# Phase one ordered by hand, h3T over hT, and values one chain later in a memory-augmented attention and mixer kernel

## The chip, the cores and the metric

The kernel runs on one core of a Trainium2 chip, in one launch. The metric is the device time in microseconds; each kernel's time is the median of several executions on the chip. TensorE (PE in the profile) multiplies matrices into PSUM; VectorE (DVE), ScalarE (ACT) and GpSimd (POOL) do the rest; SyncE (SP) only issues DMAs, and POOL issues some too. Each engine takes its instructions in the order in which they were written for it, and semaphores tie the engines together.

## The reference

x is 2048 tokens of 1024 numbers. Two branches read its layer norm: A, an attention over segments of 32 tokens with 8 memory tokens that the previous segment hands on, and B, a token-shift mixer with an MLP.

```python
def _A_ref(x, mem0, Wq, Wk, Wv, Wo, seg_len):      # 32 heads of 128
    for s in range(n_seg):
        h = jnp.concatenate([mem, x[:, s*seg_len:(s+1)*seg_len]], axis=1)
        q, k, v = (jnp.einsum('btd,dhe->bhte', h, W) for W in (Wq, Wk, Wv))
        scores = jnp.where(mask, jnp.einsum('bhqe,bhke->bhqk', q, k) * scale, -1e9)
        o = jnp.einsum('bhqk,bhke->bhqe', _softmax(scores), v)
        o = jnp.einsum('bhte,hed->btd', o, Wo)
        mem = o[:, :M]
        outs.append(o[:, M:])
def _B_ref(x, w1, w2, w3, w4):
    h = _gelu(_layernorm(x) @ w1)
    ...
    x1 = x + concat_of_four_shifted_quarters(h) @ w2
    return x1 + _gelu(_layernorm(x1) @ w3) @ w4
xn = _layernorm(x)
return x + _A_ref(xn, ...) + _B_ref(xn, ...)
```

## The kernel before

The kernel is written under a manual schedule: nothing reorders it, so the order of the program's lines is the order on each engine. It has four stages that follow one another on TensorE.

Phase one works on 16 tiles of 128 tokens. For each tile, `ln_stats` takes mean and variance on DVE and the power -0.5 on POOL; `ln_apply` (L205) normalises into `xn2` on DVE, issues the DMA transpose and the next loads on SP, and has ACT overwrite the tile `xts[n]` with its layer norm (L213). The first four tiles are transposed by TensorE against an identity (`pe_trans`, L228), with DVE copying one half out of PSUM and ACT the other. `stage1` (L246) multiplies w1 by the transposed tiles, for eight column blocks `co` of eight accumulating matmuls each, and ACT's GELU writes hTB; `seg_sums` (L240) adds up segments for branch A. The tiles go in nine groups: 1, 1, then 2 each. `warm` issues matmuls on a zero tile.

Phase two (L286) computes x1 tile by tile, 16 matmuls each, with the second layer norm `xn3`, written back to memory as R1 by POOL's queue, and transposed by DMA into xn3T through SP's queue. Between the transposes SP issues the twelve remaining loads of w3 (L309).

Phase three (L456) goes over four blocks `tb` of 512 tokens: 28 chains of eight matmuls (L461), each followed by a GELU into `h3T` (L462), then 56 chains' worth of matmuls with w4 (L479). h3T and w4 lie in a pool that is opened where phase two's pools were closed, so their memory is that of hTB, w2, the x tiles and phase two's ring.

The attention takes 32 steps, four blocks `b` of 512 tokens by eight groups `hg` of four heads. A step has twelve chains of eight matmuls (L799): four for q, four for k, four for v. Between them stands work of the step before, put there by `at(c, ...)`, after chain c: `scores(p, m)` (L565) multiplies q and k into psS, ACT takes the exponential (ET, L574), DVE makes normalised weights and lays them out as a block-diagonal matrix BD (L576 to L589); `values(p, m)` (L596) multiplies V by BD into psO, DVE adds a memory term into oX (L604), and ACT copies one column out, oTm (L608). There is one psS, one psO, three BD, and a ring of four PSUM tiles ("mm") for all chains. Step 1 of a block has the output projection of the block before (`out_chain`, L698). In block 0, `first_soft` and its companions treat the first segment.

## Time and profile before

| | us |
|---|---|
| median of 3 executions | 1581.95 |
| lowest and highest | 1572.84, 1586.62 |
| the profiled execution | 1586.39 |
| its span in the trace | 1584.6 |

Device time counts a little more than the span, which runs from the first to the last instruction. Times in the trace start at the span's start. Phase one runs from 0 to 85, phase two to 140, phase three from 140 to 560, the attention from 560 to the end. A row of a timeline gives start, duration, engine, line, operation, output <- inputs, shape and count, and in brackets the idle time before it with what ended it. A row of the waits gives who waited for whom, the sum in us, how often, and the longest.

### The profile page before, as it was taken

The page shows a single profiled execution, that of the slowest core. Times are in us where ns is not written, and L with a number is a line of the kernel's source. Part 1 is how long each engine was busy: PE and PEld are TensorE (multiplying, and loading weights), DVE is VectorE, ACT ScalarE, POOL GpSimd, SP SyncE. Part 2 cuts the span into 40 slices and gives each one's busy share as a digit, 9 for nine tenths or more (in the row PEclk, how much of TensorE's full clock was granted, in tenths as well). Part 3 has the DMA queues.
Part 4 walks back from the last instruction along what each step waited for, and adds up shares of the span by engine and source line. Part 5 has one row for each costly group of instructions (what it writes and reads, how often), then busy time and mean ns, then how long its engine had stood idle before and what let it go on. Part 6 is the DMA issues. An engine that isn't in the chain of part 4 may idle for free.

```text
span 1584.6 us, 24108 instructions
## 1 busy us (share of the span) xinstructions
PE 1525.0 (96%) x9609; PEld 793.9 (50%) x9609; DVE 667.9 (42%) x1562; ACT 460.4 (29%) x1249; POOL 232.7 (15%) x640
## 2 busy tenths in 40 slices
PE   7997999999999999999999999999999999999998
PEld 5953444444444466665544444444444444444445
DVE  6365011010110225566632666641666651566652
ACT  4632301202113024444410343420334420334320
POOL 3233010020120101212110111110111110111100
PEclk7999999999999999999999999999999999999999
DMA  5779644454220645464522454431445441344211
GB/s 154 192 199 254 218 158 135 133 199 133 73 100 22 205 136 171 134 186 141 166 84 63 133 154 140 136 112 47 133 140 153 134 129 54 110 133 133 94 32 38
DMA packets 190885, 208.38 MB, mean 132 GB/s; under 512 B 51176, under 2 KB 158712, under 8 KB 190768
## 3 DMA queue, kind: packets, MB, share of 16 engines
q1 hardware_dynamic: 183520, 182.49, 38.5%
q0 software_dynamic: 7248, 24.31, 4.3%
q8 instruction: 77, 1.26, 0.4%
q14 instruction: 40, 0.33, 0.1%
HBM read 170.07 MB, written 25.17 MB: 123 GB/s over the span
## 4 chain that ended last, share of the span: by engine, by line
PE 69%; DVE 18%; ACT 5%; issue 3%; DMA 3%; POOL 1%; SPq 0%; DVEq 0%; POOLq 0%; ACTq 0%
PE psP L698 14%; PE psV L548 12%; PE ps L479 12%; PE ps L461 12%; PE psK L541 5%; PE psQ L525 4%; ACT ET L574 4%; DVE Q L532 4%; PE ps L253 3%; DVE BD L589 3%; DVE oX L604 2%; DMA xn3T<-xn 2%; PE psO L600 1%; DVE EQ L576 1%; DVE PT L585 1%
## 5 line engine op out<-in xcount | busy, mean ns | idle before, releaser
L698 PE MATMUL psP<-wo_sb,oX 128*128 128x512 bf16 x1024 | 222.8, 379 | 0.0
L479 PE MATMUL ps<-w,h3T 128*128 128x512 bf16 x896 | 195.0, 379 | 0.0
L525 PE MATMUL psQ<-xT,w 128*128 128x512 bf16 x768 | 174.3, 379 | 0.0
L548 PE MATMUL psV<-w,xT 128*128 128x512 bf16 x768 | 173.8, 379 | 0.0
L541 PE MATMUL psK<-xT,w 128*128 128x512 bf16 x768 | 173.8, 379 | 0.0
L541 PEld LDWEIGHTS <-w 128*128 128x128 bf16 x1280 | 122.4, 98 | 90.0 <-issue 4.3
L698 PEld LDWEIGHTS <-oX 128*128 128x128 bf16 x1024 | 99.7, 98 | 118.4
L608 ACT CAST oTm<-psO 128x16 bf16<-128x16 f32 x128 | 22.9, 179 | 455.0 <-DVE oX L604 455.0
L525 PEld LDWEIGHTS <-w 128*128 128x128 bf16 x1024 | 97.7, 98 | 109.8
L462 ACT ACTIVATE h3T<-ps 128x512 bf16<-128x512 f32 x112 | 66.5, 597 | 288.8 <-PE ps L461 284.0
L574 ACT ACTIVATE ET<-psS 32x132 f32<-32x132 f32 x512 | 139.2, 272 | 4.6
L479 PEld LDWEIGHTS <-h3T 128*128 128x128 bf16 x896 | 87.2, 98 | 103.8
L548 PEld LDWEIGHTS <-xT 128*128 128x128 bf16 x768 | 74.1, 98 | 84.8
L591 POOL TENSOR_TENSOR BD<-ET,c_segone_sb 128x16 bf16<-128x16 f32 x128 | 33.7, 263 | 562.2 <-ACT ET L574 562.2
L461 PE MATMUL ps<-xn3T,w3a 128*128 128x512 bf16 x448 | 99.7, 384 | 13.4 <-ACT h3T L462 13.4
L532 DVE TENSOR_TENSOR Q<-psQ,QM 128x512 bf16<-128x512 f32 (+1 forms) x128 | 83.6, 678 | 65.0 <-ACT Q L531 40.4
L576 DVE STREAM_TRANSPOSE EQ<-ET 128x128 f32<-128x128 f32 x128 | 39.9, 311 | 164.2 <-ACT ET L574 164.2
L604 DVE TENSOR_TENSOR oX<-psO,VM 128x512 bf16<-128x512 f32 (+1 forms) x128 | 86.4, 675 | 48.2 <-PE psO L600 48.2
L549 ACT CAST V<-psV 128x512 bf16<-128x512 f32 x128 | 75.0, 586 | 99.8 <-PE psV L548 98.0
L461 PE MATMUL ps<-xn3T,w3b 128*128 128x512 bf16 x448 | 97.7, 379 | 0.0
L589 DVE TENSOR_TENSOR BD<-PT,c_segone_sb 128x512 bf16<-128x512 bf16 x128 | 89.9, 702 | 4.5
L392 DVE TENSOR_SCALAR xt<-xt,lnst 128x1024 bf16<-128x1024 bf16 x16 | 8.7, 546 | 196.9 <-POOL R L391 196.9
(149 smaller groups left out, 1558.7 us busy)
## 6 DMA issues: line engine op xcount, KB each, us to landing
w<-in_A_Wq_dram SPq DMA_DIRECT2D x32, 1024.0 KB, 5.7
w<-in_A_Wk_dram SPq DMA_DIRECT2D x32, 1024.0 KB, 5.7
w<-in_A_Wv_dram SPq DMA_DIRECT2D x32, 1024.0 KB, 5.7
R_scratch<-x POOLq DMA_DIRECT2D x16, 512.0 KB, 8.0
R<-R_scratch SPq DMA_DIRECT2D x16, 512.0 KB, 7.7
chunk<-in_A_Wv_dram SPq DMA_DIRECT2D x8, 1024.0 KB, 6.1
R_scratch<-R POOLq DMA_DIRECT2D x16, 512.0 KB, 6.7
chunk<-in_A_Wo_dram SPq DMA_DIRECT2D x8, 1024.0 KB, 6.0
```

What stands on the lines that cost most here:

```text
L461: nc.tensor.matmul(ps[:], w3[:, k, (f % FH) * P:(f % FH + 1) * P], xn3Ts[tb][:, :, k, :], start=(k == 0), stop=(k == KT - 1))
L462: nc.scalar.activation(h3T[:, f, :], ps[:], ACTF.Gelu_apprx_tanh)
L479: nc.tensor.matmul(ps[:], h3T[:, f, j * P:(j + 1) * P], w4t[f // 4][:, f % 4, ch * 512:(ch + 1) * 512], start=(f == 0), stop=(f == FT - 1))
L525: nc.tensor.matmul(ps[:], w[:, k, hh * P:(hh + 1) * P], s.xm[:, k, 0:512], start=(k == 0), stop=(k == KT - 1))
L532: nc.vector.tensor_tensor(q3[:, j0:16, 0:SEG], p3_[:, j0:16, :], QM[:, 4 * s.hg + hh, z + j0:z + 16].unsqueeze(2).to_broadcast((P, 16 - j0 ...
L541: nc.tensor.matmul(ps[:, 0:c], w[:, k, hh * P:(hh + 1) * P], s.xm[:, k, h2 * c:(h2 + 1) * c], start=(k == 0), stop=(k == KT - 1))
L548: nc.tensor.matmul(ps[:], s.xm[:, k, m * P:(m + 1) * P], w[:, k, :], start=(k == 0), stop=(k == KT - 1))
L549: nc.scalar.copy(s.V[:, m, :], ps[:])
L574: nc.scalar.activation(ET[q, :, :], ps[q, :, W * j:W * (j + 1)], ACTF.Exp, scale=SCALE)
L589: nc.vector.tensor_tensor(B4[:, :, :, 0:SEG], PT[:].unsqueeze(2).to_broadcast((P, 4, 4, SEG)), so.unsqueeze(3).to_broadcast((P, 4, 4, SEG) ...
L604: nc.vector.tensor_tensor(oX[:, hsl(s.hg), m * P:(m + 1) * P].rearrange("p h (j i) -> p h j i", i=SEG)[:, :, j0:4, :], p4[:, :, j0:4, 0:SE ...
L698: nc.tensor.matmul(ps[:], oX[:, h, m * P:(m + 1) * P], wo_sb[:, h, ch * 512:(ch + 1) * 512], start=(h == 0), stop=(h == H - 1))
```

## The change

In phase one the tiles go in eight pairs. The first pair's matmuls are split: for six column blocks the first half of w1 (k 0 to 3) is used, then tiles 2 and 3 are transposed, then the second half follows. x2 and x3 are loaded between the halves of w1. A GELU on a one-column tile is ACT's first instruction. ACT's layer norm of the x tiles becomes a call of its own, `normalise_x`. Tiles 0 and 1 are transposed through the "mm" ring, 2 and 3 through one tile of two banks. The warm matmuls read a tile of 0.5 in place of zero, are 16 in place of 13, and two more follow each of the first two transposes. Three constants are loaded in phase two. The last four loads of w3 move from phase two to the start of phase three. hT gets a pool of its own that lives until the end of phase three, and h3T is a view of it. In the attention each `values` is called one chain later, behind the next `scores`; `first_soft`, `first_trans` and `out_chain` move by one chain with it.

```diff
+    load_qones, qones = const_tile("c_qones", ..., later=True)
+    load_causal, causal = const_tile("c_causal", causal_np, F32, later=True)
+    load_mask40, mask40 = const_tile("c_mask40", _mask40(False), later=True)
...
+    ht_pool = htx.enter_context(tc.tile_pool(name="hT", bufs=1))
+    hT_all = ht_pool.tile([P, KT * (S + 4)], BF16)
+    hTB = hT_all[:].rearrange("p (k s) -> p k s", k=KT)
+    h3T = hT_all[:, 0:FT * 512].rearrange("p (f s) -> p f s", f=FT)
...
-        hTB = keep.tile([P, KT, S + 4], BF16)
...
+            nc.vector.memset(fill[:], 0.5)
+            pre = ring.tile([P, 1], F32, tag="pre")
+            nc.scalar.activation(pre[:], fill[:, 0:1], ACTF.Gelu_apprx_tanh)
...
             load_x(0)
             load_x(1)
-            for k0 in (0, 4):
-                nc.sync.dma_start(w1_sb[:, k0:k0 + 4, :], w1_v[:, k0:k0 + 4, :])
-            for n in range(2, 8):
+            load_w1(0)
+            load_x(2)
+            load_x(3)
+            load_w1(4)
+            for n in range(4, 8):
                 load_x(n)
...
+            def w1_part(g, co, ps, ks):
+                for k in ks:
+                    nc.tensor.matmul(ps, w1_sb[:, k, co * P:(co + 1) * P], xn2Ts[g][:, :, k, :], start=(k == 0), stop=(k == KT - 1))
+                if ks[-1] == KT - 1:
+                    nc.scalar.activation(hTB[:, co, 2 + g * 256:2 + g * 256 + 256], ps, ACTF.Gelu_apprx_tanh)
...
+            warm(16)
             ln_stats(0)
+            ln_stats(1)
+            ln_apply(0)
+            pe_trans(0)
+            warm(2)
+            ln_apply(1)
+            pe_trans(1)
+            warm(2)
+            normalise_x(0)
+            normalise_x(1)
+            first = [mm_tile("ps1")[:, 0:256] for _ in range(4)]
+            t = aux_tile([P, 2, 512], "A", "ps1")
+            first += [t[:, 0, 0:256], t[:, 1, 0:256]]
+            for co in range(6):
+                w1_part(0, co, first[co], range(4))
+            ln_stats(2)
+            ln_stats(3)
+            for n in (2, 3):
+                ln_apply(n)
+            for n in (2, 3):
+                pe_trans(n)
+            for co in range(6):
+                w1_part(0, co, first[co], range(4, KT))
+            stage1(0, (6, 7))
+            seg_sums(0)
+            seg_sums(1)
+            ln_stats(4)
+            for g in range(1, NT // 2):
+                nxt = [n for n in (2 * g + 2, 2 * g + 3) if n < NT]
+                for n in nxt:
+                    if n + 1 < NT:
+                        ln_stats(n + 1)
+                    ln_apply(n)
+                    dma_trans(n)
+                stage1(g, range(4))
+                if g == 1:
+                    normalise_x(2)
+                    normalise_x(3)
+                for n in nxt:
+                    normalise_x(n)
+                stage1(g, range(4, KT))
+                seg_sums(2 * g)
+                seg_sums(2 * g + 1)
...
-                if n < 12:
+                if n < 8:
                     load_w3(4 + n)
+                elif n == 8:
+                    load_qones()
+                    load_causal()
+                    load_mask40()
...
-        h3T = big.tile([P, FT, 512], BF16)
+        for i in range(12, 16):
+            load_w3(i)
...
         if pp is not None:
-            at(0, values, pp, 3)
+            at(1, values, pp, 3)
         if p is not None:
             at(0, scores, p, 0)
             for m in range(3):
-                at(3 * m + 3, values, p, m)
                 at(3 * m + 3, scores, p, m + 1)
+                at(3 * m + 4, values, p, m)
...
-            values(p, 3)
             scores(s, 0)
+            values(p, 3)
...
```

DVE, phase one, from the first tile's normalisation on. Before, tile 1 (x_102) is normalised after the statistics of tile 2 (x_103); xn2T is the transposed tile.

```order
L210 TENSOR_SCALAR xn_169<-x_101,lnst 128x1024
L236 CAST xn2T<-psT 128x512
L187 BN_STATS st<-x_103 128x6 x2
L188 BN_AGGR lnst<-st 128x2
L190 TENSOR_SCALAR ab<-lnst 128x1
L191 TENSOR_SCALAR ab<-ab,lnst 128x1
L210 TENSOR_SCALAR xn_195<-x_102,lnst 128x1024
```

After:

```order
L218 TENSOR_SCALAR xn_174<-x_101,lnst 128x1024
L250 CAST xn2T<-psT 128x512
L218 TENSOR_SCALAR xn_193<-x_102,lnst 128x1024
L250 CAST xn2T<-psT 128x512
L202 BN_STATS st<-x_103 128x6 x2
L203 BN_AGGR lnst<-st 128x2
```

Tile 1 is normalised and copied before anything is asked of tile 2.

ACT, from phase two into phase three: the last normalisations xn, then the first GELUs, with what each waits for. Before:

```order
L305 ACTIVATE xn_1890<-x_1858,nm_1888,r_1886 128x1024 [waits DVE_49,DMAHW3_49,Activation_49,Pool_49]
L305 ACTIVATE xn_1926<-x_1894,nm_1924,r_1922 128x1024 [waits DVE_49,DMAHW5_49,Activation_49,Pool_49]
L462 ACTIVATE h3T<-ps_1965 128x512 [waits DMASW5_49,DMASW6_49,DMASW4_49,DMASW7_49,DMASW3_49,DMAHW0_49,DMASW2_49,DMAHW1_49,DMASW1_49,DMAHW2_49,DMASW0_49,DMAHW6_49,DVE_49,DMAHW7_49,PE_49,Activation_49]
L462 ACTIVATE h3T<-ps_1975 128x512 [waits PE_49]
L462 ACTIVATE h3T<-ps_1985 128x512 [waits PE_49]
```

After:

```order
L341 ACTIVATE xn_1780<-x_1748,nm_1778,r_1776 128x1024 [waits DVE_49,DMAHW0_49,Activation_49,Pool_49]
L341 ACTIVATE xn_1816<-x_1784,nm_1814,r_1812 128x1024 [waits DVE_49,DMAHW1_49,Activation_49,Pool_49]
L341 ACTIVATE xn_1852<-x_1820,nm_1850,r_1848 128x1024 [waits DVE_49,DMAHW2_49,Activation_49,Pool_49]
L503 ACTIVATE hT_all<-ps_1894 128x512 [waits PE_49]
L503 ACTIVATE hT_all<-ps_1904 128x512 [waits PE_49]
```

The first GELU's waits for DMA queues (DMAHW is SP's, DMASW is POOL's) and for DVE are gone; the normalisations ahead of it still wait for DMAs.

ACT, in the attention, a steady stretch of a step with chains for K and V. Before:

```order
L574 ACTIVATE ET<-psS 32x132 x4
L542 CAST K<-psK 128x512 x3
L608 CAST oTm<-psO 128x4x4
L574 ACTIVATE ET<-psS 32x132 x4
L542 CAST K<-psK 128x512
L549 CAST V<-psV 128x512 x2
```

After:

```order
L616 ACTIVATE ET<-psS 32x132 x4
L584 CAST K<-psK 128x512
L650 CAST oTm<-psO 128x4x4
L584 CAST K<-psK 128x512 x2
L616 ACTIVATE ET<-psS 32x132 x4
L584 CAST K<-psK 128x512
```

oTm stood directly ahead of the exponentials ET; now it stands one cast behind the previous ones, with two casts between it and the next.

More of the change, by code (lines that the diff above doesn't have):

```diff
@@ L105, in const_tile @@
         t = cpool.tile(list(arr.shape), dt, name=name + "_sb")
-        nc.gpsimd.dma_start(t[:], d.ap())
+        load = lambda: nc.gpsimd.dma_start(t[:], d.ap())
+        if later:
+            return load, t
+        load()
         return t
@@ L244, in seg_sums @@
                 nc.scalar.copy(xs[:, :, 4 * n:4 * n + 4], ps[:])
-            def stage1(gi, cos):
-                n0, nt = groups[gi]
-                xn2T = xn2Ts[gi]
-                w = nt * P
-                for co in cos:
-                    ps = mm_tile("ps1")
-                    for k in range(KT):
-                        nc.tensor.matmul(ps[:, :w], w1_sb[:, k, co * P:(co + 1) * P], xn2T[:, 0:nt, k, :], start=(k == 0), stop=(k == KT - 1))
-                    nc.scalar.activation(hTB[:, co, 2 + n0 * P:2 + n0 * P + w], ps[:, :w], ACTF.Gelu_apprx_tanh)
@@ L484 @@
                     att_prep()
+    htx.close()
     specx.close()
@@ L841 @@
             out_part(b, 2, 0, hp)
+            scores(s, 3)
             values(s, 2)
-            scores(s, 3)
             out_part(b, 3, 0, hp)
```

97 lines of the change are left out of this document (38 added, 59 removed).

## The prediction

> **What bounds the kernel now.** I read the page's busy line first, then TensorE's waits, then the timeline of each place that a wait named, then the granted clock there.
>
> ```profile
> PE 1525.0 (96%) x9609; PEld 793.9 (50%) x9609; DVE 667.9 (42%) x1562; ACT 460.4 (29%) x1249; POOL 232.7 (15%) x640
> ...
> PE psO L600 <- DVE BD L589: 20.1, 37, 1.5
> PE ps L461 <- ACT h3T L462: 13.4, 1, 13.4
> PE psZT L645 <- ACT K L542: 6.1, 7, 1.1
> PE ps L253 <- ACT hTB L254: 4.7, 2, 2.6
> ```
>
> TensorE is busy for 1525.0 of 1584.6 us, so only its idle time and its slow stretches can be won. The idle time has three homes: the attention, where the weighted values (psO) wait 37 times for the block-diagonal weights BD; one hole of 13.4 us between phases two and three; and the ramp of phase one.
>
> ```profile
> 1.20 4.62 PE L182 MATMUL psW<-zero 128*128 128x512 bf16 x13 [1.20 <-DVE zero L167]
> 7.88 1.00 PE L234 MATMUL psT<-c_ident_sb,xn 128*128 128x128 bf16 x8 [2.07 <-DVE xn L210]
> 9.42 0.61 PE L253 MATMUL ps<-xn2T,w_sb 128*128 128x128 bf16 x4 [0.53 <-DMA w_sb<-in_B_w_dram]
> 12.66 3.17 PE L253 MATMUL ps<-xn2T,w_sb 128*128 128x128 bf16 x28 [2.63 <-DMA w_sb<-in_B_w_dram]
> ...
> 35.13 5.32 PE L253 MATMUL ps<-xn2T,w_sb 128*128 128x256 bf16 x32 [2.08 <-ACT hTB L254]
> ...
> 77.62 7.15 PE L253 MATMUL ps<-xn2T,w_sb 128*128 128x256 bf16 x64
> ...
> 84.60 0.54 PE L243 MATMUL psX<-c_segone_sb,x 128*128 128x4 bf16 x16
> 85.01 15.27 PE L293 MATMUL ps<-w_sb,hTB 128*128 128x512 bf16 x70
> 7.50:9.00 1.50, 1.00 (x8) 0.65 0.97 336
> 35.20:38.40 3.20, 3.20 (x17) 0.51 1.07 257
> ```
>
> Phase one ends at 85.01. In its steady part a pair of token tiles takes 85.01 - 77.62 = 7.39 us; eight pairs would be 59.1, so the ramp costs 25.9. The last two rows are clock windows (start:end, length, TensorE busy, granted clock, DMA): the clock falls in the gap after the 13 warm matmuls, and is 0.51 again for 3.2 us after the 2.08 us gap ahead of 35.13.
>
> **Part 1, phase one reordered.** The DVE work up to the first transposes is unchanged, so they still start at 7.88.
>
> ```profile
> 8.50 0.69 DVE L236 CAST xn2T<-psT 128x512 bf16<-128x512 f32 x1 [0.67 <-PE psT L234]
> 13.33 1.29 DVE L187 BATCH_NORM_STATS2 st<-x 128x6 f32<-128x512 bf16 x2 [4.14 <-DMA x<-in_A_x_dram]
> 15.22 0.54 DVE L210 TENSOR_SCALAR xn<-x,lnst 128x1024 bf16<-128x1024 bf16 x1
> 15.38 0.93 POOL L192 TENSOR_TENSOR lnst<-ab,neghalf 128x2 f32<-128x2 f32 x1 [6.75 <-DVE ab L191]
> 40.95 2.37 ACT L213 ACTIVATE x<-x,nm,lnst 128x1024 bf16<-128x1024 bf16 x2
> DMA to landing us min/median/max: 3.2/4.7/7.9
> ```
>
> The copy of tile 0 ends at 9.19. Tile 1 now follows at once: apply 0.54, transposes to copy 8.50 - 7.88 = 0.62, copy 0.69, so both tiles are there at 11.1, and the first half of w1 has landed (9.42). Six chains of four matmuls, 24 x 7.15/64 = 2.7 us, run to 13.8. x2 and x3 are now ahead of w1's second half; since that half took 12.66 - 9.42 = 3.2 us for 1 MB, x2 (256 KB) lands near 10.2, x3 near 11.0, the half near 14.3: nobody waits for it. DVE then needs 1.9 us of statistics per tile (13.33 to 15.22), so x3's are done at 14.9; POOL's power takes 0.93, apply 0.54, to 16.4; the copies of tiles 2 and 3, which share one PSUM tile, let TensorE go on at 17.7. The other 24 matmuls (2.7), 16 of the last two chains (1.8) and the segment sums (0.5) end at 22.8. Seven pairs at 7.39 are 51.7: 74.5.
>
> The new order has one stall of its own: in the first loop turn ACT normalises four tiles in a row, 2 x 2.37 = 4.7 us, between GELUs, while TensorE has only four chains (3.6 us) of PSUM ahead. With a GELU of some 0.4 us behind them that is 1.6 us: 76.1. One half-clock window as at 35.13 costs 1.7; I count 0.5 of it: 76.6. **Gain 85.0 - 76.6 = 8.4.** Ends: 10.5 without stall or slow clock; 3.5 with two slow windows and tile 5's DMA transpose landing at its 7.9 rather than 4.7.
>
> By the Trainium skill (TensorE: Matmul & The Clock Gate, "What's actually happening") the clock is judged in free-running windows of about 3.4 us and falls after an idle one. The rows disagree in part: 2.08 us of idle was enough. By the page alone my gaps of 1 to 1.7 us would cost nothing, phase one would end at 76.1, and most warm matmuls added would buy nothing; the row makes me keep 0.5.
>
> Loading the GELU table first takes a table load out of ACT's queue; what hides it after the change is the wait for x0. The three constants taken from POOL's start are not needed before the attention; at n = 8 of phase two their issues delay one x1 tile on POOL, whose transposes trail anyway. Costed at nothing.
>
> **Part 2, the hole between phases two and three.**
>
> ```profile
> 140.64 7.08 PE L461 MATMUL ps<-xn3T,w3a 128*128 128x512 bf16 x32
> 147.14 11.22 SPq L307 DMA_TRANSPOSE xn3T<-xn  x4
> 148.88 1.24 ACT L305 ACTIVATE xn<-x,nm,r 128x1024 bf16<-128x1024 f32 x1 [4.44 <-DMA xn3T<-xn]
> 154.46 1.24 ACT L305 ACTIVATE xn<-x,nm,r 128x1024 bf16<-128x1024 f32 x1 [4.34 <-DMA xn3T<-xn]
> 160.47 2.06 ACT L462 ACTIVATE h3T<-ps 128x512 bf16<-128x512 f32 x4 [4.77 <-DMA xn3T<-xn]
> 160.48 10.59 SPq L319 DMA_DIRECT2D w<-in_B_w_dram x7
> 161.12 19.32 PE L461 MATMUL ps<-xn3T,w3a 128*128 128x512 bf16 x80 [13.40 <-ACT h3T L462]
> ...
> 185.70 2.12 POOL L391 TENSOR_TENSOR R<-R,xt 128x1024 f32<-128x1024 f32 x1 [39.46 <-DMA xt<-in_A_x_dram]
> ...
> 204.44 5.78 PE L479 MATMUL ps<-w,h3T 128*128 128x512 bf16 x26
> R_scratch<-x POOLq DMA_DIRECT2D x16, 512.0 KB, 8.0
> w3b<-in_B_w_dram SPq DMA_DIRECT2D x8, 448.0 KB, 9.9
> ```
>
> TensorE fills its four PSUM tiles by 147.7 and waits for the first GELU, which waits until 160.47 for the last transpose, because h3T lies on memory that phase two's tiles release as one. Laid over hT it waits for TensorE alone. What is late next stands ahead of it on ACT: the normalisation of tile 15, at 154.46, waiting for the transpose of tile 11. Were that unmoved, the GELU would come 4.8 us earlier: the lower end. But four w3 loads leave that stretch. Transposes 10 and 11 landed 154.46 - 148.88 = 5.6 us apart, the last four 6.0 in all, 1.5 each; so 4.1 us goes to one w3 load and one R1 write, by bytes 1.9 to the load. Three of the four stood ahead of transpose 11: it lands 5.7 us earlier, 148.8, and the GELU starts at 150.0: wait near 2.9. As backlog also shrinks from tile 8 on (1.5 + 2.2 per tile against TensorE's 3.5 us, (140.64 - 85.01)/16), the wait may be nothing. I take 1.5 us and half of the slow clock after the hole: the L461 work took 204.44 - 140.64 = 63.8 against 28 chains of eight matmuls at 0.2157 us (part 3), 48.3, so 15.5 are lost now, 13.4 of them waiting. **Gain 13, ends 4.8 and 15.4.**
>
> The moved loads pass the last transposes on SP and stand ahead of w4. w3's second half is needed 14 chains (24.2 us) into phase three. w4's seven loads, R and xt took 160.48 to 185.70 = 25.2 us for 8.1 MB, so 1.8 MB more is 5.7. If the last transpose lands 14 us after phase two's end, w4 is in at 14 + 5.7 + 25.2 = 45 against a need at 48.6; if as late as now (20.1), at 51: 2.4 us late.
>
> **Part 3, weighted values one chain later.**
>
> ```profile
> L541 PE MATMUL psK<-xT,w 128*128 128x512 bf16 x768 | 173.8, 379 | 0.0
> ...
> 961.54 0.39 PE L570 MATMUL psS<-Q,K 128*128 128x132 bf16 x4
> 961.77 5.34 PE L541 MATMUL psK<-xT,w 128*128 128x512 bf16 x24
> 963.39 0.68 DVE L604 TENSOR_TENSOR oX<-psO,VM 128x512 bf16<-128x512 f32 x1
> 964.10 0.18 ACT L608 CAST oTm<-psO 128x16 bf16<-128x16 f32 x1 [5.71 <-DVE oX L604]
> 964.19 1.12 ACT L574 ACTIVATE ET<-psS 32x132 f32<-32x132 f32 x4
> ...
> 967.30 0.69 DVE L589 TENSOR_TENSOR BD<-PT,c_segone_sb 128x512 bf16<-128x512 bf16 x1
> ...
> 968.05 0.41 PE L600 MATMUL psO<-BD,V 128*128 128x132 bf16 x4 [0.94 <-DVE BD L589]
> ```
>
> Scores go out at 961.54, but ACT's exponentials stand behind oTm, which stands behind oX: BD is ready at 968.0, three chains are over at 967.1. Afterwards values have a fourth chain (8 x 0.2157 = 1.73), the next scores (0.23), and oX and oTm (0.86) no longer stand ahead of the exponentials: 2.8 us of slack against a longest wait of 1.5, so all 37 go. Each costs more than its idle: busy time runs to a matmul's modelled end, 0.379 after its start, while the next starts (5.34 - 0.379)/23 = 0.2157 after it, so 0.163 is hidden in each. 20.1 + 37 x 0.163 = **26 us.** Queued behind the new place: oTm now waits for oX, which comes after the next score chain on DVE, so ACT's K and V casts behind it slip by some 3 us; the PSUM ring holds three more chains, 5.2 us, and covers that. Upper end 33: the seven psZT waits (6.1 + 7 x 0.163) go too. Lower end 13: 0.1 us of new PSUM waits on each of 128 units.
>
> **Sum.** 8.4 + 13 + 26 = 47.4, off the profiled execution's own 1586.39: 1539.0. That execution is 4.4 over the median shown, so the same gain off the median is 1534.6; I say 1537.
>
> **The rivals.**
> A. The transposes stay late, R1 writes being the limit: part 2 gives 4.8, and w4 is 2.4 late: 1586.4 - 8.4 - 2.4 - 26 = 1550. For it: ACT waited for transposes 4.4 us even between tiles 10 and 11. Against: the last four came at 1.5 us each.
> B. ACT holds TensorE: part 3 gives 13: 1552. For it: oTm already waits for oX often. Against: ACT is busy 29%.
> C. Slower: the PSUM ring runs dry in the attention because the casts sit behind oTm, at 0.5 us in each of 128 units, 64 us, with no gain there: 1586.4 - 21.4 + 64 = 1629. It decides from 21.4/128 = 0.17 us a unit. Against: ring slack of 5.2 us above a slip of 3.
> D. Values are not what is awaited, and another wait stands right behind: part 3 gives nothing, 1565. Against: in the row above nothing else was late but BD.
>
> **How the numbers follow.** Forecast 0.64, A 0.15, B 0.12, C 0.04, D 0.05. A change within 1% (16 us) could not be told from none. Faster by more holds the forecast, A, B and most of D: 0.92; same 0.05; slower 0.03. All low ends together give 1565, all high ends 1528 off the profile and 1524 off the median; the range 1522 to 1558 takes in A and B, and leaves out C, D and the worst sums.
>
> **What would show it.** Phase two starts near 77 and no ACT row normalises later than 36; the wait of L502 for ACT falls below 4 us; the psO rows under TensorE's waits vanish, ET starts within 0.5 us of psS, and steps of blocks one to three take 12 x 1.73 + 8 x 0.23 = 22.6 us. I am wrong if psK, psV or psQ rows appear there waiting for ACT, or if the phase-four matmuls wait for w4.

## The result

The changed kernel takes 1535.32 us (median of four executions, 1534.35 to 1536.46), the kernel before 1582.23 beside it (four executions, 1572.84 to 1586.62): a ratio of 0.9711, interval 0.9667 to 0.9756. The profiled execution took 1536.46, its span is 1534.7. The prediction of 1537, from 1522 to 1558, holds the time. The two profiled executions differ by 49.9 us, the medians by 46.9: the kernel before was profiled in one of its longer executions, so the table of stages below is a little kind to the change.

The busy line of the changed kernel's page:

```profile
PE 1514.3 (99%) x9552; PEld 793.2 (52%) x9552; DVE 662.4 (43%) x1562; ACT 450.5 (29%) x1241; POOL 231.9 (15%) x640
```

TensorE is busy for all but 20.4 us of the span; before it was all but 59.6. The chain that ended last runs on it for 93% of the span (69% before). What it still waits for (who waited for whom, sum in us, how often, longest):

```profile
PE psT L247 <- DVE xn L218: 3.6, 3, 2.2
PE psQ L567 <- DVE Q L574: 2.4, 7, 0.4
PE psT L247 <- DVE xn2T L250: 1.9, 2, 1.1
PE ps L262 <- ACT hT_all L264: 1.9, 2, 1.4
...
PE psO L642 <- ACT oTm L650: 1.0, 1, 1.0
PE psZT L687 <- ACT K L584: 0.9, 3, 0.3
```

Of the 37 waits of the weighted values (psO) for BD none is left, of the seven psZT waits a seventh of the time, and the hole of 13.4 us ahead of phase three (ps waiting for the GELU) is not in the list at all. The seven psQ waits for Q (2.4 us) are new; seven psK waits for the same Q (2.2 us) went. What is left lies mostly in phase one.

Cut at the first matmul of each stage, the two spans give this; the first chains of phase three with w3 stand for its first block:

| stage | before, us | after, us | gain | predicted |
|---|---|---|---|---|
| phase one | 85.01 | 81.55 | 3.5 | 8.4 (3.5 to 10.5) |
| phase two | 55.63 | 55.62 | 0 | 0 |
| phase three, w3 of its first block | 63.80 | 48.36 | 15.4 | 13 (4.8 to 15.4) |
| the rest of phase three | 355.19 | 355.19 | 0 | 0 |
| attention | 1024.97 | 993.98 | 31.0 | 26 (13 to 33) |
| span | 1584.6 | 1534.7 | 49.9 | 47.4 |

**Phase one.** TensorE's timeline of the changed kernel, where the first pair's second half begins:

```profile
15.80 0.61 PE L247 MATMUL psT<-c_ident_sb,xn 128*128 128x128 bf16 x4 [2.22 <-DVE xn L218]
17.53 0.59 PE L247 MATMUL psT<-c_ident_sb,xn 128*128 128x128 bf16 x4 [1.12 <-DVE xn2T L250]
18.79 0.58 PE L247 MATMUL psT<-c_ident_sb,xn 128*128 128x128 bf16 x4 [0.67 <-ACT xn2T L252]
20.15 0.58 PE L247 MATMUL psT<-c_ident_sb,xn 128*128 128x128 bf16 x4 [0.78 <-DVE xn2T L250]
20.53 4.47 PE L262 MATMUL ps<-xn2T,w_sb 128*128 128x256 bf16 x20
...
37.23 7.15 PE L262 MATMUL ps<-xn2T,w_sb 128*128 128x256 bf16 x64 [1.39 <-ACT hT_all L264]
...
81.55 2.75 PE L329 MATMUL ps<-w_sb,hT_all 128*128 128x512 bf16 x12
```

Three things are to be seen. The transposes of tiles 2 and 3 come in four groups, one after the other, each but the first waiting for the copy of the group before it: they write one PSUM tile, and the second half waits for the first half's copy. Then 20 matmuls take 4.47 us, twice the 2.2 that 20 take elsewhere (7.15/64 each). And at 37.23 stands the stall behind four normalisations, 1.39 us where 1.6 was worked out. The clock row (start:end, length, TensorE busy, granted clock, DMA) says why the 20 were slow:

```profile
15.80:26.00 10.20, 7.15 (x39) 0.50 0.06 14
```

**The boundary.** The changed kernel's ACT, SP and TensorE there:

```profile
140.35 1.24 ACT L341 ACTIVATE xn<-x,nm,r 128x1024 bf16<-128x1024 f32 x1 [2.45 <-POOL nm L339]
141.50 1.66 ACT L503 ACTIVATE hT_all<-ps 128x512 bf16<-128x512 f32 x3
...
118.58 24.31 SPq L343 DMA_TRANSPOSE xn3T<-xn  x8
142.95 2.03 SPq L155 DMA_DIRECT2D w3b<-in_B_w_dram  x4
145.48 12.65 SPq L360 DMA_DIRECT2D w<-in_B_w_dram  x7
...
137.17 24.35 PE L502 MATMUL ps<-xn3T,w3a 128*128 128x512 bf16 x112
161.36 24.34 PE L502 MATMUL ps<-xn3T,w3b 128*128 128x512 bf16 x112
```

The last normalisation waits for no transpose (nm is the tile's own statistics), the first GELU starts 4.3 us after phase three's first matmul, and 224 matmuls run through. w3's second half and w4 are there in time. The experiments show below that this is one of two faces of the boundary.

**The attention.** One step of the changed kernel, TensorE and then ACT:

```profile
928.72 0.39 PE L612 MATMUL psS<-Q,K 128*128 128x132 bf16 x4
928.95 1.89 PE L583 MATMUL psK<-xT,w 128*128 128x512 bf16 x8
930.68 0.40 PE L642 MATMUL psO<-BD,V 128*128 128x132 bf16 x4
...
933.67 0.18 ACT L650 CAST oTm<-psO 128x16 bf16<-128x16 f32 x1 [2.20 <-DVE oX L646]
...
935.05 1.12 ACT L616 ACTIVATE ET<-psS 32x132 f32<-32x132 f32 x4
```

Scores, a chain, values, and no idle time in brackets on TensorE. Outside block 0 most steps without an output projection take 22.57 us (921.35 to 943.92 is one), as worked out; the first of block 1 takes 24.2, the third of each of these blocks 22.8.

### The profile page after: what moved, and what is told of

Its sections match the earlier page's. It is cut to its first block, busy times and chain, and to the rows that moved or that the text cites. A ratio compares the mean times of both kernels' runs of the same rounds, so it can differ in the third digit from the quotient of the medians.

```text
span 1534.7 us, 23988 instructions
## 1 busy us (share of the span) xinstructions
PE 1514.3 (99%) x9552; PEld 793.2 (52%) x9552; DVE 662.4 (43%) x1562; ACT 450.5 (29%) x1241; POOL 231.9 (15%) x640
## 4 chain that ended last, share of the span: by engine, by line
PE 93%; DVE 4%; ACT 1%; DMA 1%; issue 0%; SPq 0%; POOL 0%; ACTq 0%; DVEq 0%
PE psP L740 14%; PE psV L590 14%; PE psK L583 13%; PE ps L502 13%; PE ps L520 13%; PE psQ L567 12%; PE ps L329 4%; PE ps L262 3%; PE psO L642 2%; PE psS L612 2%; PE psM L599 1%; ACT ET L616 1%; DVE Q L574 1%; DMA x<-in_A_x_dram 1%; DVE BD L631 1%; PE psY L762 1%
## 5 line engine op out<-in xcount | busy, mean ns | idle before, releaser
L520 PE MATMUL ps<-w,hT_all 128*128 128x512 bf16 x896 | 195.0, 379 | 0.0
L567 PE MATMUL psQ<-xT,w 128*128 128x512 bf16 x768 | 178.1, 379 | 0.4 <-DVE Q L574 0.4
L590 PE MATMUL psV<-w,xT 128*128 128x512 bf16 x768 | 177.6, 379 | 0.0
L583 PE MATMUL psK<-xT,w 128*128 128x512 bf16 x768 | 177.5, 379 | 0.0
L503 ACT ACTIVATE hT_all<-ps 128x512 bf16<-128x512 f32 x112 | 66.7, 597 | 283.9 <-PE ps L502 283.9
L520 PEld LDWEIGHTS <-hT_all 128*128 128x128 bf16 x896 | 87.1, 98 | 103.8
L502 PE MATMUL ps<-xn3T,w3a 128*128 128x512 bf16 x448 | 97.7, 379 | 0.0
L502 PE MATMUL ps<-xn3T,w3b 128*128 128x512 bf16 x448 | 97.7, 379 | 0.0
L746 DVE TENSOR_TENSOR ot<-psP,Rt 128x512 bf16<-128x512 f32 x32 | 22.0, 691 | 156.2 <-PE psP L740 156.2
```

The source lines that it names most:

```text
L502: nc.tensor.matmul(ps[:], w3[:, k, (f % FH) * P:(f % FH + 1) * P], xn3Ts[tb][:, :, k, :], start=(k == 0), stop=(k == KT - 1))
L503: nc.scalar.activation(h3T[:, f, :], ps[:], ACTF.Gelu_apprx_tanh)
L520: nc.tensor.matmul(ps[:], h3T[:, f, j * P:(j + 1) * P], w4t[f // 4][:, f % 4, ch * 512:(ch + 1) * 512], start=(f == 0), stop=(f == FT - 1))
L567: nc.tensor.matmul(ps[:], w[:, k, hh * P:(hh + 1) * P], s.xm[:, k, 0:512], start=(k == 0), stop=(k == KT - 1))
L583: nc.tensor.matmul(ps[:, 0:c], w[:, k, hh * P:(hh + 1) * P], s.xm[:, k, h2 * c:(h2 + 1) * c], start=(k == 0), stop=(k == KT - 1))
L590: nc.tensor.matmul(ps[:], s.xm[:, k, m * P:(m + 1) * P], w[:, k, :], start=(k == 0), stop=(k == KT - 1))
```

## The experiments

Each is the changed kernel with one edit, unless said otherwise. Cut in the same way, their profiled executions give this table; every one of them has 55.6 us for phase two and 355.2 for the rest of phase three.

| run | phase one | w3, first block | attention | median us (executions) |
|---|---|---|---|---|
| changed kernel | 81.55 | 48.36 | 993.98 | 1535.32 (4) |
| e1_old_values | 80.33 | 59.62 | 1024.23 | 1566.51 (8) |
| e2_first_old | 79.49 | 56.03 | 996.76 | 1539.52 (4) |
| e3_swap_only | 80.24 | 57.62 | 1020.02 | 1560.97 (10) |
| e4_w3_in_p2 | 80.25 | 50.78 | 994.04 | 1537.62 (1) |
| e5_h3T_own | 80.22 | 60.08 | 993.48 | 1546.47 (1) |
| e6_two_tiles | 78.50 | 48.36 | 993.82 | 1533.35 (1) |
| e7_fill_gap | 78.03 | 48.35 | 993.49 | 1532.49 (1) |
| e8_norm_early | 79.24 | 48.36 | 994.19 | 1534.35 (1) |
| e10_best | 75.46 | 60.22 | 993.90 | 1537.49 (6) |
| e11_old_boundary | 79.84 | 63.19 | 993.85 | 1549.95 (4) |
| e12_w3_in_p2 | 79.87 | 59.75 | 993.55 | 1545.77 (4) |
| e13_h3T_own | 80.36 | 64.22 | 993.41 | 1542.41 (4) |

Two columns move on their own. Eight of the experiments have the changed kernel's phase one unedited, and with it they make nine traces from 79.49 to 81.55, median 80.24: the changed kernel's profile was the longest of the nine, so phase-one edits are held against 80.24 below. Each of those edits has one trace, and the nine scatter from 0.75 below to 1.3 above their median. And the first block of phase three is long in kernels that have the changed kernel's boundary word for word; that is taken up under the boundary.

### The attention

**The old order.** All of the attention's edits undone:

```diff
-            at(1, values, pp, 3)
+            at(0, values, pp, 3)
...
+                at(3 * m + 3, values, p, m)
                 at(3 * m + 3, scores, p, m + 1)
-                at(3 * m + 4, values, p, m)
...
-            at(2, first_soft, p)
-            at(6, first_trans, p)
+            at(1, first_soft, p)
+            at(5, first_trans, p)
...
-                at(1, out_chain, s.b - 1, c)
+                at(0, out_chain, s.b - 1, c)
...
```

> The changed kernel with the whole order of the attention as it was before (values one chain earlier, the first softmax, the first transposes and the output chains at their old places); phases one to three as changed. Theory (the values waited for BD, and moving them is worth the whole 31.0 us by which the attention became shorter): 1535.3 + 31 = 1566 us, attention 1025 us from the first psQ to the end, some 37 waits of psO for BD. Rival one (part of the 31 comes from elsewhere, for instance from phase three ending in better order, so that only my 26 or fewer belong to the order): 1555 to 1561 us, attention 1014 to 1020. Rival two (the attention's gain is that of a better clock or of transfers and not of the order): within 5 us of 1535. Phase two starts at 81.5 and phase three's first block is 48.4 us long in each case.

1566.51 us, and the attention takes 1024.23, within 0.8 of the kernel before. The waits of the kernel before are back:

```profile
PE psO L642 <- DVE BD L631: 20.1, 37, 1.5
...
PE psZT L687 <- ACT K L584: 6.1, 7, 1.1
...
PE psK L583 <- DVE Q L574: 2.2, 7, 0.4
```

So the theory holds: the order of the attention is worth 30.3 us in the traces and 31.2 between the medians. The sum over the waits agrees: psO, psZT and psK waited 28.4 us in 51 places, the changed kernel's attention waits 4.8 us in 12 (psQ, psO, psZT and one of 0.5), so 23.6 went, and 39 x 0.163 us that a modelled end hides (6.4) makes 30.0.

**Which part of the order.** In the next, only the first segment's work goes back; in the one after it, the values go back to their old chain too, but stay behind the scores:

```diff
-            at(2, first_soft, p)
-            at(6, first_trans, p)
+            at(1, first_soft, p)
+            at(5, first_trans, p)
```

> The changed kernel with only the first softmax and the first transposes of a block back at their old chains (1 and 5 in place of 2 and 6); the values stay late. The 31.0 us of the attention are 5 more than the 26 worked out for the psO waits, and the psZT waits for the K cast went too (7 x 1.1 us before). Theory: those seven waits belong to the values' old place, the first softmax's place is worth little: 1535 to 1537 us, psZT waits stay at 0.3 us. Rival: the later first softmax and transposes gave the extra 5 us: about 1540 us, with seven psZT waits of about 1 us or waits of the first psO of a block for BD.

```diff
-        if pp is not None:
-            at(1, values, pp, 3)
...
             at(0, scores, p, 0)
+            if pp is not None:
+                at(0, values, pp, 3)
             for m in range(3):
                 at(3 * m + 3, scores, p, m + 1)
-                at(3 * m + 4, values, p, m)
+                at(3 * m + 3, values, p, m)
```

> The changed kernel with the values, the first softmax, the first transposes and the output chains back at their old chains, but the values still behind the next scores instead of ahead of them. Theory (two things make BD late, the order with the scores, worth 0.86 us for oX and oTm plus 0.23 for the scores, and the missing chain of 1.73 us): of the before's waits only what is longer than 1.1 us stays, 37 x 0.4 at 1.5 us each, so 12 to 16 us of psO waits remain: 1548 to 1553 us. Rival one (the order with the scores is all that matters): 1535 to 1538. Rival two (the extra chain is all that matters): 1562 to 1567, psO waits near 20 us.

The first takes 1539.52 us, and its attention 996.76, 2.8 longer. That is nearer to the rival's time, but the waits are of neither: psK waits for ACT's K cast, and the old psZT waits are gone.

```profile
PE psK L583 <- ACT K L584: 5.0, 8, 0.9
```

The second takes 1560.97, 26 us longer in the attention, and fits none of the three. Its waits:

```profile
PE psZT L687 <- ACT K L584: 10.3, 7, 2.1
PE psQ L567 <- ACT VZ L667: 8.0, 7, 1.2
PE psV L590 <- ACT K L584: 7.4, 7, 1.1
```

No row in which psO waits for BD: putting the values behind the scores is enough to end that. My count of 37 x 0.4 left over was wrong; 30 of the 37 waits of the kernel before, 17.7 us of the 20.1, come after 860 us and are at most 1.1 us long, and the swap was counted to give 1.1; the one of 1.5 us went too. There most steps take 22.57 us, as in the changed kernel (953.98 to 976.55 is one). Of the 26.0 us, 23.8 are in block 0, whose eight steps take 234.5 us here, 218.7 in the old order and 210.6 in the changed kernel, from its first q chain to that of block 1. One of its steps, ACT and then TensorE:

```profile
642.75 1.12 ACT L616 ACTIVATE ET<-psS 32x132 f32<-32x132 f32 x4
647.04 0.18 ACT L650 CAST oTm<-psO 128x16 bf16<-128x16 f32 x1 [3.18 <-DVE oX L646]
647.11 1.22 ACT L584 CAST K<-psK 128x260 bf16<-128x260 f32 x4
...
642.70 3.71 PE L583 MATMUL psK<-xm,w 128*128 128x260 bf16 x32
647.55 0.25 PE L687 MATMUL psZT<-c_ident_sb,PZ 40*40 40x40 bf16 x4 [1.14 <-ACT K L584]
```

oTm stands on ACT directly behind the exponentials and waits 3.18 us for oX, which DVE does behind the whole softmax of these scores; the K casts stand behind oTm. In block 0 a K chain takes 0.9 us (3.71 for four) and not 1.7, so the four PSUM tiles are full at 646.4 and the first cast comes at 647.11. That is the queue of the prediction's rivals B and C, casts behind oTm, which I had put in every step; here block 0 is 23.8 us longer and the rest 2.2. The psQ waits for VZ come the same way: in this step ACT casts VZ at 639.88, behind an oTm that waited 3.31 us for oX. The same step in the changed kernel, ACT:

```profile
626.84 1.12 ACT L616 ACTIVATE ET<-psS 32x132 f32<-32x132 f32 x4
627.98 0.65 ACT L584 CAST K<-psK 128x260 bf16<-128x260 f32 x2
631.25 0.18 ACT L650 CAST oTm<-psO 128x16 bf16<-128x16 f32 x1 [2.62 <-DVE oX L646]
```

oTm still waits 2.62 us for oX, but since it is asked for one chain later, two K casts pass ahead of it. That is what the extra chain buys, and nearly only in block 0: most steps elsewhere are equal without it. Block 1 as a whole is 1.3 us shorter with it (237.7 against 239.1), block 2 0.8 (236.1 against 236.9), block 3 0.1.

### The boundary of phases two and three

**One half undone each.** The last four w3 loads back among the transposes (h3T stays over hT), and h3T in memory of its own pool again (the loads stay moved), each as a single profiled execution (e4, e5) and again over four executions (e12, e13):

```diff
-                if n < 8:
+                if n < 12:
                     load_w3(4 + n)
-                elif n == 8:
+                if n == 8:
...
-        for i in range(12, 16):
-            load_w3(i)
```

> The changed kernel with the last four loads of w3 back among phase two's transposes (tiles 8 to 11); h3T stays on the memory of hT. Theory (the hole between phases two and three had two causes, the memory of h3T and these loads, which hold transpose 11 and so ACT's normalisation of tile 15): phase three's first block takes 48.4 + 5 to 10 us, the wait of L502 for ACT comes back with 5 to 10 us, and the kernel takes 1540 to 1546. Rival (the memory alone was the cause, the loads are off the path): block of 48.4 us, no wait, 1535 to 1537.

> The kernel of e4 (last four w3 loads among phase two's transposes, h3T over hT) once more and timed. Theory (by the one look, where the wait was 2.3 us, the loads matter little once h3T lies over hT): median 1536 to 1539. Rival (the look was a lucky one and the loads hold transpose 11 as I predicted): median 1540 to 1546.

```diff
-    hT_all = ht_pool.tile([P, KT * (S + 4)], BF16)
-    hTB = hT_all[:].rearrange("p (k s) -> p k s", k=KT)
-    h3T = hT_all[:, 0:FT * 512].rearrange("p (f s) -> p f s", f=FT)
...
+        hTB = keep.tile([P, KT, S + 4], BF16)
...
+        h3T = big.tile([P, FT, 512], BF16)
```

> The changed kernel with h3T in memory of its own pool again, which phase two's tiles release, and hT kept as before; the last four loads of w3 stay moved behind phase two. Theory (h3T's first GELU waits for the last transposes, which now land about 145 us, 8 us after phase two's end at 137.2, and TensorE has four PSUM tiles, 7 us, ahead): a wait of 1 to 3 us of L502 for ACT, phase three's first block 49.5 to 52 us. Rival one (the memory carried the hole alone): the full 13.4 us back, block 62 to 64. Rival two (the moved loads carried it alone): no wait, 48.4.

> The kernel of e5 (h3T in its own pool's memory, last four w3 loads behind phase two) once more and timed. Theory (the first GELU waits for all sixteen transposes, 152.5 - 148.7 = 3.7 us behind the last normalisation in the one look, where the transposes came late as well): median 1537 to 1541. Rival (the memory carries nearly the whole hole): median 1544 to 1548.

And both undone:

> The changed kernel with the whole boundary of phases two and three as before: h3T in its own pool's memory and the last four loads of w3 among phase two's transposes. Theory (the edit of the boundary is worth what the medians leave, 46 less 31 of the attention and 3.5 of phase one): median 1545 to 1548, single executions from 1537 to 1551, first block of phase three 56 to 64 us. Rival (the hole depends on the execution's DMA pace and the edit is worth only some 4 us, the part of the wait of the one look at h3T in its own memory that lies behind the last normalisation): median 1538 to 1541.

Single executions say more than the medians. With the loads back: 1534.54, 1537.62, 1545.76, 1545.78, 1545.93. With h3T in its own memory: 1537.19, 1538.50, 1546.32, 1546.47, 1550.59. With both: 1545.98, 1549.79, 1550.11, 1552.47. The changed kernel's four: 1534.35 to 1536.46. So either half alone reaches within 0.2 and 2.8 us of the changed kernel in its best executions, and is 9 to 13 us longer than its own best in three of five; with both undone no execution came within 9 us of the changed kernel. Nearly all of the expectations missed. E4's execution (first block 50.78, a wait of 2.3) lies between its theory and its rival; e12's median, 1545.77, is its rival's; e5's block of 60.08 fits none of its three, and e13's 1542.41 neither of its two. They asked for one time each, and most executions fall into one of two groups some 10 us apart. The theory of e11 (1545 to 1548) is 2 too low, its rival is out; its trace has a wait of 12.8 us ahead of phase three.

What are the two groups? The changed boundary has both too. The old-order kernel has it word for word, and its profiled execution shows the hole. TensorE and ACT:

```profile
135.96 7.08 PE L502 MATMUL ps<-xn3T,w3a 128*128 128x512 bf16 x32
151.28 20.29 PE L502 MATMUL ps<-xn3T,w3a 128*128 128x512 bf16 x80 [8.24 <-ACT hT_all L503]
...
142.72 1.24 ACT L341 ACTIVATE xn<-x,nm,r 128x1024 bf16<-128x1024 f32 x1 [5.04 <-DMA xn3T<-xn]
149.50 1.24 ACT L341 ACTIVATE xn<-x,nm,r 128x1024 bf16<-128x1024 f32 x1 [5.54 <-DMA xn3T<-xn]
150.65 2.04 ACT L503 ACTIVATE hT_all<-ps 128x512 bf16<-128x512 f32 x4
```

The last normalisations wait for transposes, as in rival A, and the GELU comes behind them. The block is 11.3 us longer than the changed kernel's; 8.2 of that is the wait, and TensorE's clock is granted at 0.50 for 10.2 us from 146.9 on. Counted over the changed boundary, executions more than 5 us above the lowest of their kernel are none of 4 in the changed kernel, 2 of 8 in e1, 1 of 4 in e2, 3 of 10 in e3 and 3 of 6 in e10: 9 of 32. In four of the nine a trace shows the hole (8.2, 5.4, 7.4 and 8.9 us); of the rest only the time is known. The single profiled executions of e6, e7 and e8 have this boundary too, and no hole. So four of eight profiled executions have it and, by their time, five of 27 others: whether taking the trace has a hand in it is not shown.

What differs is the DMA. The two queues from 120 to 140 us, hardware (transposes, but for the end of a w3 load) and software (the R1 writes), with packets, MB and their share of the 16 engines' time, in the changed kernel

```profile
q1 hardware_dynamic: 7401, 2.26, 63.2%
q0 software_dynamic: 1120, 3.82, 51.9%
```

and in e1:

```profile
q1 hardware_dynamic: 3722, 1.35, 63.1%
q0 software_dynamic: 842, 2.82, 53.8%
```

For the same share half as many packets get through on the hardware queue: 0.632 x 16 x 20 / 7401 = 27 ns each against 54 ns. The two queues' shares add up to 115% and 117%, so packets overlap on an engine, and these times hold what one packet waits for another. The two programs are the same up to there but for the attention's later order, so what sets the pace is not in the edit. The transposes then land up to 17.1 us after their issue, where the changed kernel's land within 9.4. The eight traces of this boundary sort alike: without a hole (changed kernel, e6, e7, e8) 24 to 38 ns a packet and all transposes landed within 12.2 us, with one (e1, e2, e3, e10) 45 to 58 ns and the slowest at 16.5 to 17.5. Why an execution takes the one pace or the other stays open; no run here varied it alone, and to take R1's writes out of the way was not tried.

The Trainium skill (Advanced Engine Details and Errata, "X-Bar Transpose (TRN2)" under "DMA Advanced Topics") says that transpose DMAs are as fast as regular ones. No run here has transposes alone, so none tests that; beside the R1 writes, by the rows above, a MB on the transposes' queue took 28% of the engines' time in the changed kernel's execution and 47% in the other, a MB of R1 writes 14% and 19%, waiting included.

The profiled execution of h3T in its own memory with the longest hole shows the two parts in one place, ACT of e13:

```profile
148.33 1.24 ACT L338 ACTIVATE xn<-x,nm,r 128x1024 bf16<-128x1024 f32 x1 [4.56 <-DMA xn3T<-xn]
155.55 2.06 ACT L501 ACTIVATE h3T<-ps 128x512 bf16<-128x512 f32 x4 [5.98 <-DMA xn3T<-xn]
```

Late transposes hold the normalisation to 148.33, which no edit here takes away; h3T's memory adds 5.98 behind it. So the view over hT takes away 3.7 us (the same wait in e5) to 6.5 (in e11) behind the last normalisation, and in an execution whose transposes come late TensorE's wait of 5 to 9 us for the late normalisations stays. That the moved loads are worth anything alone is not shown: by their times e12, with the loads back, has the hole in three of four executions, and e10, with them moved and timed beside it, in three of six.

### Phase one

**Two PSUM tiles.** The halves of tiles 2 and 3 go through two tiles, and the first pair has four column blocks ahead of them in place of six:

```diff
-                    t = aux_tile([P, 2, 512], "B", "psT")
-                    ps = [t[:, 0, :], t[:, 1, :]]
+                    ps = [aux_tile([P, 512], "A", "psT")[:], aux_tile([P, 512], "B", "psT")[:]]
...
-            for co in range(6):
+            for co in range(4):
...
-            stage1(0, (6, 7))
+            stage1(0, (4, 5, 6, 7))
```

> The changed kernel with the transposes of tiles 2 and 3 written through two separate PSUM tiles (one per half) instead of two banks of one tile; the first pair of tiles is split over four column blocks in place of six, to make room. Theory (in the changed kernel the second half of each tile waits for the copy of the first half out of the shared tile, 1.12 and 0.78 us, and the second tile for both): the four transpose groups become two, waits of 0.6 to 1.2 us go, and pair 1 starts 2 to 3 us earlier than 28.3; phase two starts at 78.5 to 79.5, if the clock falls as there. Rival (four column blocks instead of six leave less work ahead, so TensorE idles longer for tile 2 and nothing is won): phase two starts at 81 to 82.

```profile
14.88 0.85 PE L246 MATMUL psT<-c_ident_sb,xn 128*128 128x128 bf16 x8 [2.30 <-DVE xn L218]
16.60 1.01 PE L246 MATMUL psT<-c_ident_sb,xn 128*128 128x128 bf16 x8 [0.88 <-DVE xn2T L249]
```

Four groups become two, pair 1 starts at 25.27 in place of 28.31, phase two at 78.50. As expected, but x2 landed 0.9 us earlier in this execution (its statistics start at 10.53, against 11.45); against 80.24 the gain is 1.7, and 78.50 is 1.0 below the shortest of the nine.

**The gap filled.** Ten warm matmuls ahead of the transposes of tile 2:

```diff
+            warm_b(10)
             ln_stats(2)
             ln_stats(3)
```

> The changed kernel with ten more warm matmuls (2.2 us) in the gap ahead of the transposes of tile 2. Theory (the half clock from 15.7 to 26.1 comes from the gap of 2.22 us there, and costs 2.5 to 3 us): the clock stays at 1.0 through phase one, the 20 matmuls that took 4.47 us take 2.2, and phase two starts at 78.5 to 79. Rival one (the four small gaps of 0.7 to 1.1 us between the transposes drop the clock by themselves): the clock falls some us later and phase two starts at 80.5 to 82. Rival two (the half clock is hidden by ACT or DVE): the clock stays up and phase two starts at 81.5 all the same.

```profile
13.62 2.10 PE L202 MATMUL psW<-fill 128*128 128x512 bf16 x9
...
19.39 2.35 PE L267 MATMUL ps<-xn2T,w_sb 128*128 128x256 bf16 x20
```

```profile
15.70:26.10 10.40, 7.63 (x85) 1.00 0.17 30
```

The clock stays at 1.00, the 20 matmuls take 2.35, and phase two starts at 78.03: 2.2 us against 80.24, 3.5 against the changed kernel's own trace. The theory holds; the small gaps between the transposes alone did not drop the clock in this run.

**Normalising earlier.** x2 and x3 normalised ahead of the transposes of tiles 2 and 3:

```diff
             for n in (2, 3):
+                normalise_x(n)
+            for n in (2, 3):
                 pe_trans(n)
...
-                if g == 1:
-                    normalise_x(2)
-                    normalise_x(3)
```

> The changed kernel with ACT's normalisation of x2 and x3 moved ahead of the transposes of tiles 2 and 3, so that in the first loop turn two and not four normalisations stand in a row. Theory: the wait of 1.39 us of TensorE for the GELU at 37.2 goes, and phase two starts at 80.0 to 80.3. Rival (the normalisations now hold the copies of tiles 2 and 3 on ACT: 4.7 us of work against the 5.1 us that ACT idles there, begun only when x3's statistics are in): the copies come 2 to 4 us later and phase two starts at 82 to 85.

The wait of 1.39 us is gone, but a copy on ACT now comes later (the third transpose group waits 1.35 for it, not 0.67); phase two starts at 79.24, 1.0 us less than 80.24 but only 0.25 below the shortest of the nine traces. Theory right in kind, and the rival costs it a part; the size is not clear of the scatter.

**Together.** Both halves transposed before the first copy, the ten warm matmuls, and x2 and x3 normalised at the end of the first pair:

```diff
                 for h in range(2):
                     p3_ = ps[h].rearrange("p (k t) -> p k t", k=4)
                     for k in range(4):
                         nc.tensor.matmul(...)
+                for h in range(2):
+                    p3_ = ps[h].rearrange("p (k t) -> p k t", k=4)
                     dst = xn2Ts[n // 2][:, n % 2, 4 * h:4 * h + 4, :]
...
+            warm_b(10)
             ln_stats(2)
             ln_stats(3)
...
             stage1(0, (6, 7))
+            normalise_x(2)
+            normalise_x(3)
...
-                if g == 1:
-                    normalise_x(2)
-                    normalise_x(3)
```

> The changed kernel with three edits in phase one: both halves of tiles 2 and 3 are transposed before the first is copied out, ten warm matmuls fill the gap ahead of tile 2, and ACT normalises x2 and x3 at the end of the first pair and not in the first loop turn. Theory (the changed kernel's phase one loses 3.5 us to the half clock, about 1.3 to the halves that wait for copies in the shared tile, 1.4 to the four normalisations in a row): phase two starts at 75 to 76 in place of 81.5, and the kernel takes 1528.5 to 1530. Rival one (the three overlap, so that only the filled gap counts): phase two at 77.5 to 78.1, 1531.5 to 1532.5. Rival two (DMA, the transposes of later tiles, becomes the limit when phase one is shorter): the pairs of the loop take more than 7.39 us, waits of L262 for DMA, 1533 to 1535. The boundary of phases two and three is the changed kernel's; if its hole comes and goes with the pace of the transposes, one or two of ten executions are 5 to 10 us longer.

```profile
17.77 0.61 PE L252 MATMUL psT<-c_ident_sb,xn 128*128 128x128 bf16 x8 [1.40 <-ACT xn2T L259]
...
75.46 14.84 PE L336 MATMUL ps<-w_sb,hT_all 128*128 128x512 bf16 x66
```

Phase one is as short as the theory has it: 75.46, 4.8 us less than 80.24, about what e6, e7 and e8 gain one by one (1.7 + 2.2 + 1.0). Its fastest execution, 1529.95, is 4.4 below the changed kernel's fastest. But its six executions are 1529.95, 1530.67, 1534.44, 1540.54, 1540.87 and 1542.15: half have the hole by their time (8.9 us in the profiled one), not one or two of ten, so the median is 1537.49 and not the 1528.5 to 1530 expected, the ratio to the kernel before 0.9711 (0.9678 to 0.9744), the same as the changed kernel's. As a kernel it is not shown to be faster; its phase one is.

None of the change's own edits in phase one was undone. What the pairs, the split first pair, the early table load, and the 16 warm matmuls in place of 13 with two behind each transpose are worth one by one was not tried; the 3.5 and 4.8 us compare with one trace of the kernel before.

## Why the prediction was right, and where it was not

**Part 1, mis-sized: 8.4 us predicted, 3.5 in the profiled pair, 4.8 by the median of nine traces.** The table load, the loads between the halves and the split chains came as worked out: the first 24 matmuls run from 10.79 where 11.1 was predicted. The stall of 1.6 us was there (1.39). Two terms failed. "The copies of tiles 2 and 3, which share one PSUM tile, let TensorE go on at 17.7" counted the copies, but not that the second half's transposes wait for the first half's copy: TensorE went on at 20.53, 2.8 us later, 0.5 of it because tile 3's normalised tile came at 16.9 and not at 16.4. And "one half-clock window ... I count 0.5 of it" was too small: 20 matmuls at half clock cost 2.2 us alone. E6 takes the first away, e7 the second, e10 both. The measured 3.5 stands at the low end of the range, but not for the reasons given there: the half clock lasted 10.2 us in one piece, three times as long as the one at 35.13, and tile 5's transpose held nothing in this trace. Nor do its terms give 3.5: 76.1 with two windows of 1.7 and 3.2 for the later transpose is 82.7, a gain of 2.3, unless part of the 3.2 hides behind the stall.

The sentence on the clock rule was half right. By the Trainium skill (TensorE: Matmul & The Clock Gate, "What's actually happening") the windows are free-running and some 3.4 us long; the traces agree with that: the same four transpose groups lead to 3.4 us of half clock in e2's execution (18.8 to 22.2) and to 10.2 in the changed kernel's, and in e4 to 6.8, one, three and two windows. The Trainium skill's condition, an idle window, does not hold here if it means one without any work: the gap ahead of the changed kernel's fall was 2.22 us, and e2's longest 1.65.

**Part 2, right in the profiled pair, 13 against 15.4; the reason was half the story.** With the normalisations on time the wait was nothing, which was the upper end. What I took for the kernel's own backlog also depends on the pace of the transposes in the execution, and rival A, at 0.15, happens in 9 of 32 executions of this boundary: in the four that have a trace part 2 gives 3.6 to 7.8 us, against A's 4.8. Its late w4 did not come (the rest of phase three is 355.2 in all), and that R1's writes are the limit is not shown. The edit matters all the same: undone, none of four executions was, by its time, without the hole, and their median is 14.6 us above the changed kernel's four, none of which had it. Against e10's median, timed beside them with the hole in three of six, and allowing for its phase one (4.8), it is 7.7. The moved loads were in time, as worked out.

**Part 3, right, 26 against 31.0.** The sum took the 37 psO waits; the psZT waits went too (5.2 of 6.1 us), which was the case of the upper end; psK's seven for Q only became psQ's seven. The slack worked out for the swap alone, 1.1 us, was just enough outside block 0 (e3), so the fourth chain was not needed there. In block 0 it was, against late casts on ACT: the queue of rivals B and C is real where the PSUM ring of four holds 3.7 us of chains and not 6.9, and the fourth chain nearly ends its cost. In the changed kernel neither B nor C came, nor D.

**The sum, in part luck.** The parts were off by -4.9, +2.4 and +5.0 us in the profiled pair, and these nearly cancel: 49.9 against 47.4. None of the changed kernel's four executions met the slow transposes, which 9 of 32 did by their time. (All high ends together give 1523 off the median, not 1524.)

**The signs.** Phase two starts at 81.55, not 77. "No ACT row normalises later than 36" was my mistake: ACT normalises two tiles in every turn of the loop, to 73. L502 waits for nothing in the profile. The psO rows are gone but one of 1.0, late in the last block, for oTm. ET starts 0.5 to 1.1 us after psS in the step at 921.35, a little later than I said. The steps take 22.57 against 22.6. Of the signs of being wrong, one psQ row waits for ACT (VZ, 0.5 us, in block 0), none in blocks one to three, and no matmul with w4 waits.

## What to carry to other kernels

When a wait is removed by putting a consumer later, look at what the consumer's own results then stand ahead of on the next engine: the swap alone ended every wait for BD and made block 0 16 us longer than it had been, because a small cast that waits for DVE stood ahead of the casts that empty the PSUM ring. In this kernel two halves written into one PSUM tile with a copy between them are serial, though two engines copy; write both, then copy. And where a stage hangs on busy DMA queues, time it over several executions before a part of the change is credited: here single executions of one program differ by up to 14.6 us.

## What the runs showed of the hardware that was not expected

- The pace of DMA transposes beside plain writes differs by a factor of two between executions of the same stage, 27 and 54 ns a packet, waiting included, at the same share of the engines.
- The half clock in phase one lasted 3.4 us in one trace, 6.8 in seven and 10.2 in one with the same code; the first ended phase one earliest, at 79.49, the last latest, at 81.55. In the last x2 also came latest, with statistics from 11.45 against 10.61 to 11.35 in the others.
